# Attention and two MLP layers on one core: the order of work at the layer change, three gate subtracts and one conversion step on other engines

## The chip, the cores and the metric

One core of one Trainium2 chip runs the whole program. The metric is the device time of one execution in microseconds (us), as the median of several runs. The core has five engines, each working through its own queue in order: TensorE (matmuls, PE in the profile), VectorE (DVE), ScalarE (ACT), GpSimd (POOL) and SyncE (SP, which here issues all DMAs).

## The reference

Attention with a compressive memory, whose output of 2304 tokens by 512 goes through two MLP layers. Cut to what is computed:

```python
# q, k, v: 4 x 8 heads x 576 x 64; causal softmax attention 'local', and a memory read 'mem_out'
x = g * mem_out + (1 - g) * local            # -> 2304 x 512
h = x @ w_in                                 # layer one, 512 -> 2048
x = (h * (1 / (1 + exp(-1.702 * h)))) @ w_out
h = x @ w_in2                                # layer two
out = (h * clip(h + 3, 0, 6) / 6) @ w_out2
```

The four weight matrices come as float64, the rest as float32.

## The kernel before

The 2304 tokens are six tiles of 384 (`TILES`, NT = 384), kept transposed, so that a tile is four pieces of 128 x 384 (KD = 4, index kk or d). The hidden dimension is cut in NF = 16 parts, index f. A *unit* is (layer, tile, f): layer one's six tiles with sixteen parts each, then layer two's. The function `moe` walks through the units. For each unit it issues the h product (lines 302 to 304), starts the gate, and then issues the y product (lines 282 to 284) of an earlier unit, so that the gate has time.

Every factor is split into a rounded float32r half and a rest, and a product is three matmuls of 128 x 128 by 128 x 384: weight half by data half, weight rest by data half, weight half by data rest. So h takes 12 matmuls (four quarters kk of three), and y takes 12 (three for each output piece d, summed over f in four banks).

*The gate* of one unit (`gate`) is four instructions: an activation of h on ScalarE (line 254 for layer one, a tanh; 258 for layer two, a relu), a VectorE instruction that multiplies by h (256, 260), a cast on ScalarE to the half `g[:, 0]` (263), and a subtract that gives the rest `g[:, 1]` (265). The subtract is on VectorE for layer one's first tile and on GpSimd for all others (`GLE`).

*The splits of x* (`split_x`, lines 247 and 248) are the same cast on ScalarE and subtract on VectorE, one pair for each quarter. The buffers of the split x exist once, so a split of the next tile waits until the h product of f = 15 has read that quarter. They are asked for by `after_quarter`: for the next tile of layer one and, after layer one's last tile, for layer two's first tile at f = 15; for layer two at f = 12.

*The weights* come as float64 words, and `conv_w` makes a half and a rest of each block of 128 x 512: on VectorE lines 197 and 202 (shift and merge of the two 32-bit words, in place), on GpSimd line 206 (add the constant STEP to the high word read as a float), on ScalarE line 208 (Abs of the low word; part of layer one's are done on VectorE, line 210) and line 212 (Sign of the high word less STEP), on VectorE line 215 (min and multiply), on ScalarE line 222 (cast to the half), and line 225 (the rest; on VectorE for layer two). There are 64 such conversions, 32 for each layer. Layer two's are issued one in every 7 steps of the stream (`PR`; a unit has 8 steps), from layer one's last tile on.

The code makes chains of these steps as generators, which advance by one step at each `chains.step()`. A step of layer two's conversions is kept behind the last gate's instruction on the same engine (`after_gates` with CB = 0). What the code gives is a priority; the program is built with a planner that plays the instructions through with its own durations and fixes the order on each engine, so the order on an engine is not the order of the code.

From layer one's last tile on (`LAG` = 3), y runs three units behind h, h has three banks, and g has four buffers. So when layer one's last h product is issued, y of f = 12 follows, and y of f = 13, 14 and 15 wait in `pend`; they are issued behind h of layer two's f = 0, 1 and 2.

Of the kernel before, what the change touches and what calls it, by code (L numbers as in the profile page):

```python
# [8 lines left out]
F32 = mybir.dt.float32  # L9
F32R = mybir.dt.float32r  # L10
I32 = mybir.dt.int32
AF = mybir.ActivationFunctionType
ALU = mybir.AluOpType
# [6 lines left out]
KD = DM // 128  # L20
NF = DFF // 128
# [18 lines left out]
DPIN = (1, 0, 0, 0, 0, 1)  # L40
NR = ((1,), (1,), (1,), (1,), (1,), (1,))
GLE = (0, 1, 1, 1, 1, 1, 1)
XEV = (0,)
PC = ((1, 6, 11), 8)
W0 = (2, 3)
# [18 lines left out]
STEP = 768.0  # L64
# [12 lines left out]
def f32(ap):  # L77
    return ap.bitcast(F32)
# [26 lines left out]
def attention_moe_kernel(ctx: ExitStack, tc: tile.TileContext, qk0, sk0, sk1, vm0, vm1, bb, w1, w2, out):  # L105
    nc = tc.nc
    PE, ACT, DVE, POOL, SP = nc.tensor, nc.scalar, nc.vector, nc.gpsimd, nc.sync

    const = ctx.enter_context(tc.tile_pool(name="const", bufs=1))
# [8 lines left out]
    chains = Chains()  # L118
# [11 lines left out]
    gated = {"DVE": [], "ACT": [], "POOL": []}  # L130
# [51 lines left out]
    def conv_w():  # L182

        n = w_at[1]
        key = layer, f, a = w_jobs[n]
        if n >= 4 and w_jobs[n - 4] in w_gen:
            chains.finish(w_gen[w_jobs[n - 4]])
        w_at[1] += 1
        load_w(w_at[1])
        if layer == 0:  # L190
            load_w(min(2 * NF, w_at[1] + AHEAD))
        z = 2 if layer == 1 else int(2 * f + a >= 2 * PRE)
        words = w_raw.pop(key).rearrange("p (n two) -> p n two", two=2)
        lo, hi = words[:, :, 0], words[:, :, 1]

        def chain():
            first = DVE.tensor_scalar(
                out=lo, in0=lo, scalar1=29, scalar2=0x40000000, op0=ALU.logical_shift_right, op1=ALU.bitwise_or
            )
            if PIN[layer]:  # L200
                tc.keep_in_program_order(first)
            DVE.scalar_tensor_tensor(
                out=lo, in0=hi, scalar=3, in1=lo, op0=ALU.logical_shift_left, op1=ALU.bitwise_xor
            )
            yield
            POOL.tensor_scalar(out=f32(hi), in0=f32(hi), scalar1=STEP, scalar2=1.0, op0=ALU.add, op1=ALU.mult)  # L206
            if (2 * f + a) % ABS[z][1] < ABS[z][0]:
                ACT.activation(out=f32(lo), in_=f32(lo), func=AF.Abs)
            else:
                DVE.tensor_scalar(out=lo, in0=lo, scalar1=0x7FFFFFFF, scalar2=None, op0=ALU.bitwise_and)  # L210
            yield
            ACT.activation(out=f32(hi), in_=f32(hi), func=AF.Sign, bias=step_down[:, 0:1])  # L212
            yield
            x = temp(layer, f, a)
            DVE.scalar_tensor_tensor(  # L215
                out=x, in0=f32(lo), scalar=BIG, in1=f32(hi), op0=ALU.min, op1=ALU.mult
            )
            pool, tag = slot(layer, f, a)
            t = pool.tile([128, 2, DM], F32R, tag=tag, bufs=1, name=f"w{f}{a}")
            wt[key] = t  # L220
            yield
            ACT.copy(out=t[:, 0], in_=x)  # L222
            yield
            e = "DVE" if (2 * f + a) % WLE[z][1] < WLE[z][0] else "POOL"
            {"DVE": DVE, "POOL": POOL}[e].tensor_tensor(out=t[:, 1], in0=x, in1=f32(t[:, 0]), op=ALU.subtract)  # L225

        w_gen[key] = chains.start(after_gates(chain(), CB[layer]))

    def convert_to(n):
# [14 lines left out]
    def split_x(key, kk):  # L244
        r = xr.pop((key, kk))
        t = xp.tile([128, 2, NT], F32R, tag=f"xs{kk}", name=f"xs{kk}")
        ACT.copy(out=t[:, 0], in_=r)  # L247
        DVE.tensor_tensor(out=t[:, 1], in0=r, in1=f32(t[:, 0]), op=ALU.subtract)
        xs[key, kk] = t

    def gate(layer, ti, h, g):
        t = gp.tile([128, NT], F32, tag="t", bufs=GB, name="t")
        if layer == 0:
            ACT.activation(out=t, in_=h, func=AF.Tanh, scale=0.851)  # L254
            yield
            d = DVE.scalar_tensor_tensor(out=t, in0=t, scalar=1.0, in1=h, op0=ALU.add, op1=ALU.mult)  # L256
        else:
            ACT.activation(out=t, in_=h, func=AF.Relu, bias=three[:, 0:1])  # L258
            yield
            d = DVE.scalar_tensor_tensor(out=t, in0=t, scalar=6.0, in1=h, op0=ALU.min, op1=ALU.mult)  # L260
        gated["DVE"].append(d.ins)
        yield
        gated["ACT"].append(ACT.copy(out=g[:, 0], in_=t).ins)  # L263
        yield
        d = (DVE, POOL)[GLE[ti if layer == 0 else -1]].tensor_tensor(out=g[:, 1], in0=t, in1=f32(g[:, 0]), op=ALU.subtract)  # L265
        gated[("DVE", "POOL")[GLE[ti if layer == 0 else -1]]].append(d.ins)

    def moe(units, before_h, after_quarter, finish):


        pend = []

        def emit_y():
            layer, ti, f, g, gen = pend.pop(0)
            chains.finish(gen)
            w = need_w(layer, f, 1)
            if f == 0:
                for d in range(KD):
                    ys[d] = psy.tile([128, NT], F32, tag=f"y{d}", name=f"y{d}")
            for d in range(KD):  # L280
                o = d * 128
                PE.matmul(ys[d], lhsT=w[:, 0, o:o + 128], rhs=g[:, 0], start=(f == 0), stop=False)  # L282
                PE.matmul(ys[d], lhsT=w[:, 1, o:o + 128], rhs=g[:, 0], start=False, stop=False)  # L283
                PE.matmul(ys[d], lhsT=w[:, 0, o:o + 128], rhs=g[:, 1], start=False, stop=(f == NF - 1))  # L284
                if f == NF - 1:
                    finish(layer, ti, d, ys[d])
                chains.step()
                if d == KD - 1 and layer == 0 and ti == LAST:
                    load_w(2 * (NF + EARLY + f + 1))
                yield layer, ti, f  # L290

        ys = [None] * KD
        for layer, ti, f in units:
            before_h(layer, ti, f)
            w = need_w(layer, f, 0)
            h = phase["h"].tile([128, NT], F32, tag=phase["tag"], bufs=phase["bufs"], name="h")
            for kk in range(KD):
                x = xs[(layer, ti), kk]
                c = kk * 128
                behind = phase["behind"]() if kk % EVERY == 0 else None  # L300
                with tc.issue_after(behind) if behind is not None else ExitStack():
                    PE.matmul(h, lhsT=w[:, 0, c:c + 128], rhs=x[:, 0], start=(kk == 0), stop=False)  # L302
                PE.matmul(h, lhsT=w[:, 1, c:c + 128], rhs=x[:, 0], start=False, stop=False)  # L303
                PE.matmul(h, lhsT=w[:, 0, c:c + 128], rhs=x[:, 1], start=False, stop=(kk == KD - 1))  # L304
                after_quarter(layer, ti, f, kk)
                if kk < KD - 1:
                    chains.step()
                    yield layer, ti, f
            g = phase["g"].tile([128, 2, NT], F32R, tag="g", bufs=phase["lag"] + 1, name="g")
            gen = chains.start(gate(layer, ti, h, g))  # L310
            chains.step()
            yield layer, ti, f
            pend.append((layer, ti, f, g, gen))
            while len(pend) > phase["lag"]:
                yield from emit_y()
        while pend:
            yield from emit_y()
# [420 lines left out]
    with ExitStack():  # L738
# [3 lines left out]
        for _ in range(WARM):  # L742
# [6 lines left out]
            out=mask[:, 384:512], in_=mask[:, 384:512], pattern=[[-1, 128]], compare_op=ALU.is_ge,  # L749
# [6 lines left out]
        POOL.memset(three, 3.0)  # L756
        step_down = const.tile([128, 1], F32, name="step_down")
        POOL.memset(step_down, -STEP)

        gall = const.tile([128, 4, H], F32, name="gall")  # L760
        omg = const.tile([128, H], F32, name="omg")
# [16 lines left out]
        LAST = len(TILES) - 1  # L778
        units = [(layer, ti, f) for layer in range(2) for ti in range(len(TILES)) for f in range(NF)]
# [10 lines left out]
        def before_h(layer, ti, f):  # L790
            if layer == 0 and f == NF - 1 and ti < LAST:
                pump(1 << 30)
            if layer == 1 and f == 2:
                load_x2(ti + 1)

        def after_quarter(layer, ti, f, kk):
            if layer == 0 and f == NF - 1:
                split_x((0, ti + 1) if ti < LAST else (1, 0), kk)
            elif layer == 1 and f == NF - 4 and ti < LAST:
                split_x((1, ti + 1), kk)  # L800

        def load_x2(ti):
            if ti > LAST:
# [3 lines left out]
                move(4, out=r, in_=x2d[ti, d])  # L807
                xr[(1, ti), d] = r

        stream = moe(units, before_h, after_quarter, finish)  # L810

        with tc.tile_pool(name="ap", bufs=2) as ap:
            temps[:] = [ap, TWB[0]]
# [12 lines left out]
            qi, ti = 0, 0  # L826
            for layer, t, f in stream:
                if t != ti:
                    ti, qi = t, 0
# [79 lines left out]
```

## Time and profile before

| | us |
|---|---|
| median of 3 runs | 1082.98 (1082.46 to 1084.0) |
| the profiled execution, its own time | 1084.36 |
| its span, first to last instruction | 1082.5 |
| mean granted TensorE clock | 0.98 of full speed |
| TensorE busy | 1033.4 (95%) |
| VectorE busy | 510.2 (47%) |
| ScalarE busy | 498.8 (46%) |
| GpSimd busy | 399.1 (37%) |

The times of the profile count from the first instruction. In the stretch up to about 600 us attention and layer one run together; from there to about 740 us layer one's last tile and layer two's first tile run while layer two's weights are converted; after that layer two has only its products and gates. "PEclk" is the clock that was granted to TensorE, as a share of 2.4 GHz; a matmul's end is modelled, and matmuls overlap, so the number of matmuls in a stretch says more than TensorE's busy share. A gate or conversion is followed by its line number through the engines. "Idle before" is time in which the engine stood still just ahead of an instruction, and the name behind the arrow is what it waited for last.

### The profile page before, as it was taken

The page shows a single profiled execution, that of the slowest core. Times are in us where ns is not written, and L with a number is a line of the kernel's source. Part 1 is how long each engine was busy: PE and PEld are TensorE (multiplying, and loading weights), DVE is VectorE, ACT ScalarE, POOL GpSimd, SP SyncE. Part 2 cuts the span into 40 slices and gives each one's busy share as a digit, 9 for nine tenths or more (in the row PEclk, how much of TensorE's full clock was granted, in tenths as well). Part 3 has the DMA queues.
Part 4 walks back from the last instruction along what each step waited for, and adds up shares of the span by engine and source line. Part 5 has one row for each costly group of instructions (what it writes and reads, how often), then busy time and mean ns, then how long its engine had stood idle before and what let it go on. Part 6 is the DMA issues. An engine that isn't in the chain of part 4 may idle for free. (4 is left out here: it accounts for less than half of the span.)

```text
span 1082.5 us, 16719 instructions
## 1 busy us (share of the span) xinstructions
PE 1033.4 (95%) x6153; PEld 940.3 (87%) x6153; DVE 510.2 (47%) x1372; ACT 498.8 (46%) x1152; POOL 399.1 (37%) x444
## 2 busy tenths in 40 slices
PE   7877888999999999999999997998999999999998
PEld 4566766888888888888889997998999999999998
DVE  6999997344544443333444598873121121211210
ACT  6757655334454454433333566764233232332322
POOL 4778765223333333222322454543222222222221
PEclk9888998999999999999999998999999999999999
DMA  6643321211121110211110684001010010100000
GB/s 227 239 158 103 127 69 36 68 45 59 28 76 37 38 55 25 59 30 60 30 30 16 246 324 140 30 1 59 1 31 30 1 59 1 31 30 1 30 1 29
DMA packets 29280, 71.91 MB, mean 66 GB/s; under 512 B 3600, under 2 KB 12816, under 8 KB 29200
## 3 DMA queue, kind: packets, MB, share of 16 engines
q1 hardware_dynamic: 29200, 70.86, 19.7%
q8 instruction: 48, 0.79, 0.3%
q14 instruction: 32, 0.26, 0.1%
HBM read 61.41 MB, written 9.44 MB: 65 GB/s over the span
## 5 line engine op out<-in xcount | busy, mean ns | idle before, releaser
L265 POOL TENSOR_TENSOR g<-t,g 128x384 fp32r<-128x384 f32 x176 | 185.1, 1052 | 473.1 <-ACT g L263 448.5
L302 PE MATMUL h<-xs,w 128*128 128x384 f32 x768 | 267.1, 348 | 16.1 <-DVE t L256 8.1
L282 PE MATMUL y<-g,w 128*128 128x384 f32 x768 | 260.4, 340 | 3.4 <-ACT g L263 3.3
L303 PE MATMUL h<-xs,w 128*128 128x384 f32 x768 | 260.1, 339 | 0.3 <-DVE w L225 0.3
L304 PE MATMUL h<-xs,w 128*128 128x384 f32 x768 | 260.3, 339 | 0.0
L283 PE MATMUL y<-g,w 128*128 128x384 f32 x768 | 259.2, 337 | 0.0
L284 PE MATMUL y<-g,w 128*128 128x384 f32 x768 | 244.1, 339 | 0.6 <-POOL g L265 0.6
L260 DVE SCALAR_TENSOR_TENSOR t<-t,h 128x384 f32<-128x384 f32 x96 | 53.1, 553 | 273.2 <-ACT t L258 273.2
L302 PEld LDWEIGHTS h<-xs,w 128*128 128x128 f32 x768 | 146.3, 191 | 24.7 <-DVE t L256 12.6
L282 PEld LDWEIGHTS y<-g,w 128*128 128x128 f32 x768 | 145.1, 189 | 7.0 <-ACT g L263 4.6
L284 PEld LDWEIGHTS y<-g,w 128*128 128x128 f32 x768 | 142.3, 188 | 6.7 <-issue 4.1
L303 PEld LDWEIGHTS h<-xs,w 128*128 128x128 f32 x768 | 146.6, 191 | 1.4 <-issue 0.8
L304 PEld LDWEIGHTS h<-xs,w 128*128 128x128 f32 x768 | 146.0, 190 | 1.1 <-issue 0.5
L283 PEld LDWEIGHTS y<-g,w 128*128 128x128 f32 x768 | 145.1, 189 | 1.4 <-issue 1.3
L263 ACT CAST g<-t 128x384 fp32r<-128x384 f32 x192 | 98.4, 513 | 95.1 <-DVE t L260 49.2
L258 ACT ACTIVATE t<-h,three 128x384 f32<-128x384 f32 x96 | 55.7, 580 | 170.5 <-PE h L304 170.5
L454 POOL TENSOR_SCALAR p<-p,st,omg 128x128 f32<-128x128 f32 (+3 forms) x128 | 91.8, 729 | 99.3 <-DVE st L450 44.7
L446 ACT ACTIVATE p<-s,st 128x256 f32<-128x256 f32 (+4 forms) x160 | 82.4, 521 | 69.6 <-DVE st L441 57.5
L441 DVE CUSTOM_DVE_ANT_0 s<-s,mask 128x128 f32<-128x128 f32 (+3 forms) x144 | 72.6, 526 | 85.0 <-PE s L381 84.1
L256 DVE SCALAR_TENSOR_TENSOR t<-t,h 128x384 f32<-128x384 f32 x96 | 52.7, 550 | 74.5 <-ACT t L254 70.3
L381 PE MATMUL s<-qk 64*128 64x256 f32 (+5 forms) x384 | 72.3, 466 | 12.2 <-issue 3.5
L254 ACT ACTIVATE t<-h 128x384 f32<-128x384 f32 x96 | 46.7, 490 | 67.9 <-PE h L304 65.1
(79 smaller groups left out, 1103.5 us busy)
## 6 DMA issues: line engine op xcount, KB each, us to landing
r<-in_w_dram SPq DMA_DIRECT2D x64, 512.0 KB, 6.2
vm<-in_vm_dram SPq DMA_DIRECT2D x16, 386.0 KB, 3.0
qk<-in_qk_dram SPq DMA_DIRECT2D x16, 384.0 KB, 3.5
qk<-in_sk_dram SPq DMA_DIRECT2D x32, 192.0 KB, 3.3
x2d<-yo SPq DMA_DIRECT2D x24, 192.0 KB, 1.9
xr<-x2d SPq DMA_DIRECT2D x24, 192.0 KB, 3.1
out_dram<-yo SPq DMA_DIRECT2D x24, 192.0 KB, 1.9
vm<-in_vm_dram SPq DMA_DIRECT2D x16, 258.0 KB, 2.7
```

The source lines that it names most:

```text
L263: gated["ACT"].append(ACT.copy(out=g[:, 0], in_=t).ins)
L265: d = (DVE, POOL)[GLE[ti if layer == 0 else -1]].tensor_tensor(out=g[:, 1], in0=t, in1=f32(g[:, 0]), op=ALU.subtract)
L282: PE.matmul(ys[d], lhsT=w[:, 0, o:o + 128], rhs=g[:, 0], start=(f == 0), stop=False)
L283: PE.matmul(ys[d], lhsT=w[:, 1, o:o + 128], rhs=g[:, 0], start=False, stop=False)
L284: PE.matmul(ys[d], lhsT=w[:, 0, o:o + 128], rhs=g[:, 1], start=False, stop=(f == NF - 1))
L302: PE.matmul(h, lhsT=w[:, 0, c:c + 128], rhs=x[:, 0], start=(kk == 0), stop=False)
L303: PE.matmul(h, lhsT=w[:, 1, c:c + 128], rhs=x[:, 0], start=False, stop=False)
L304: PE.matmul(h, lhsT=w[:, 0, c:c + 128], rhs=x[:, 1], start=False, stop=(kk == KD - 1))
L381: ins = PE.matmul(out, **args).ins
L441: DVE.tensor_tensor_reduce(out=o, in0=o, in1=m, scale=-SCALE, scalar=init, op0=ALU.add, op1=ALU.min, accum_out=out)
L446: return ACT.activation(out=dst, in_=o, func=AF.Exp, scale=-1.0, bias=m, accum_out=s)
L454: (DVE, POOL)[e[norms[0] % len(e)]].tensor_scalar(out=dst, in0=dst, scalar1=s, scalar2=w, op0=ALU.mult, op1=ALU.mult)
```

## The change

Three edits. (1) The splits of x for layer two's first tile are no longer asked for by the quarters of layer one's last h product. When the stream comes to layer two's first unit, a new function `between` asks for all four, and then all y products that still wait (f = 13, 14, 15) are issued, ahead of layer two's first h product. (2) In layer one's last tile the gate's subtract of the last three parts (`GLL` = 3, so f = 13, 14, 15) is on VectorE and no longer on GpSimd. (3) In layer two's conversions the step constant is added on ScalarE, as an Identity activation with a bias tile, and no longer on GpSimd; the bias tile is set once at the start.

```diff
+GLL = 3
...
-            POOL.tensor_scalar(out=f32(hi), in0=f32(hi), scalar1=STEP, scalar2=1.0, op0=ALU.add, op1=ALU.mult)
+            if layer == 0:
+                POOL.tensor_scalar(out=f32(hi), in0=f32(hi), scalar1=STEP, scalar2=1.0, op0=ALU.add, op1=ALU.mult)
+            else:
+                ACT.activation(out=f32(hi), in_=f32(hi), func=AF.Identity, bias=step_up[:, 0:1])
...
-    def gate(layer, ti, h, g):
+    def gate(layer, ti, f, h, g):
...
-        d = (DVE, POOL)[GLE[ti if layer == 0 else -1]].tensor_tensor(out=g[:, 1], in0=t, in1=f32(g[:, 0]), op=ALU.subtract)
-        gated[("DVE", "POOL")[GLE[ti if layer == 0 else -1]]].append(d.ins)
+        e = "POOL" if GLE[ti if layer == 0 else -1] and not (layer == 0 and ti == LAST and f >= NF - GLL) else "DVE"
+        d = {"DVE": DVE, "POOL": POOL}[e].tensor_tensor(out=g[:, 1], in0=t, in1=f32(g[:, 0]), op=ALU.subtract)
+        gated[e].append(d.ins)
...
         for layer, ti, f in units:
+            if (layer, ti, f) == (1, 0, 0):
+                between()
+                while pend:
+                    yield from emit_y()
             before_h(layer, ti, f)
...
+        step_up = const.tile([128, 1], F32, name="step_up")
+        POOL.memset(step_up, STEP)
...
         def after_quarter(layer, ti, f, kk):
-            if layer == 0 and f == NF - 1:
-                split_x((0, ti + 1) if ti < LAST else (1, 0), kk)
+            if layer == 0 and f == NF - 1 and ti < LAST:
+                split_x((0, ti + 1), kk)
...
+        def between():
+
+            for kk in range(KD):
+                split_x((1, 0), kk)
```

## Rows read from the trace of the kernel before

**Rows 1.** Windows: busy us of PE, PEld, DVE, ACT, POOL; clock, DMA, GB/s

```profile
616.00:738.00 122.00, 113.86 (x632) 110.54 (x631) 102.84 (x150) 84.27 (x151) 61.81 (x57) 0.97 0.35 125
...
654.00:674.00 20.00, 14.15 (x65) 12.43 (x64) 15.37 (x24) 12.81 (x24) 8.63 (x8) 0.83 0.39 129
...
730.00:742.00 12.00, 9.03 (x39) 7.82 (x38) 8.59 (x14) 7.60 (x16) 3.88 (x4) 0.86 0.10 27
...
742.00:1082.00 340.00, 337.14 (x1945) 336.82 (x1944) 52.48 (x96) 106.05 (x201) 81.97 (x81) 1.00 0.07 23
```

**Rows 2.** Timeline of TensorE: start, duration, instruction, in brackets idle before, releaser

```profile
656.53 0.33 PE L304 MATMUL h<-xs,w 128*128 128x384 f32 x1
...
660.54 0.45 PE L282 MATMUL y<-g,w 128*128 128x384 f32 x1 [1.60 <-ACT g L263]
...
661.74 0.44 PE L284 MATMUL y<-g,w 128*128 128x384 f32 x1 [0.57 <-POOL g L265]
...
666.02 0.69 PE L302 MATMUL h<-xs,w 128*128 128x384 f32 x1 [3.67 <-ACT xs L247]
...
669.69 0.52 PE L304 MATMUL h<-xs,w 128*128 128x384 f32 x1
...
671.33 0.33 PE L284 MATMUL y<-g,w 128*128 128x384 f32 x1
```

**Rows 3.** Timeline of ScalarE, same columns

```profile
668.43 0.49 ACT L247 CAST xs<-xr 128x384 fp32r<-128x384 f32 x1
...
668.83 0.48 ACT L254 ACTIVATE t<-h 128x384 f32<-128x384 f32 x1
```

**Rows 4.** Waits of VectorE, 616 to 738 us; total us, times, longest

```profile
DVE wt L215 <- ACT r L212: 11.4, 9, 2.3
...
DVE t L260 <- ACT t L258: 2.9, 4, 1.3
```

**Rows 5.** Waits of ScalarE, 616 to 738 us

```profile
ACT r L212 <- POOL r L206: 6.0, 10, 1.0
```

**Rows 6.** Groups by line, 616 to 738 us; busy us, mean ns, idle before

```profile
L202 DVE SCALAR_TENSOR_TENSOR r<-r 128x512 int32<-128x512 int32 x30 | 35.3, 1190 | 0.1
...
L225 DVE TENSOR_TENSOR w<-wt,w 128x512 fp32r<-128x512 f32 x30 | 23.9, 806 | 2.7 <-ACT w L222 2.7
...
L212 ACT ACTIVATE r<-r,step_down 128x512 f32<-128x512 f32 x30 | 22.8, 768 | 6.2 <-POOL r L206 6.0
...
L215 DVE SCALAR_TENSOR_TENSOR wt<-r 128x512 f32<-128x512 f32 x30 | 22.6, 760 | 11.4 <-ACT r L212 11.4
```

**Rows 7.** Four lines alone, 616 to 738 us; duration min/median/max, ns

```profile
L202 DVE SCALAR_TENSOR_TENSOR r<-r x30: 678/1498/1511, 617.3 to 731.8; 128x512 int32<-128x512 int32 x30
...
L206 POOL TENSOR_SCALAR r<-r x30: 642/1025/1110, 618.8 to 733.4; 128x512 f32<-128x512 f32 x30
...
L215 DVE SCALAR_TENSOR_TENSOR wt<-r x30: 677/684/1137, 622.6 to 734.8; 128x512 f32<-128x512 f32 x30
...
L225 DVE TENSOR_TENSOR w<-wt,w x30: 678/682/1503, 625.5 to 736.2; 128x512 fp32r<-128x512 f32 x30
```

**Rows 8.** Timeline of all engines around one conversion

```profile
655.30 1.50 DVE L202 SCALAR_TENSOR_TENSOR r<-r 128x512 int32<-128x512 int32 x1
...
656.84 0.68 ACT L208 ACTIVATE r<-r 128x512 f32<-128x512 f32 x1 [0.81 <-DVE r L202]
...
657.95 0.75 ACT L212 ACTIVATE r<-r,step_down 128x512 f32<-128x512 f32 x1 [0.43 <-POOL r L206]
...
660.57 1.11 POOL L265 TENSOR_TENSOR g<-t,g 128x384 fp32r<-128x384 f32 x1 [2.66 <-ACT g L263]
...
660.75 1.49 DVE L202 SCALAR_TENSOR_TENSOR r<-r 128x512 int32<-128x512 int32 x1
```

**Rows 9.** Groups by line over the whole span

```profile
L265 DVE TENSOR_TENSOR g<-t,g 128x384 fp32r<-128x384 f32 x16 | 11.6, 728 | 0.0
...
L611 ACT ACT_TABLE_LOAD x1 | 1.3, 1283 | 0.7 <-PEq L892 0.7
```

More of the change, by code (lines that the diff above doesn't have):

```diff
@@ L264, in gate, with moe @@
         yield
-        d = (DVE, POOL)[GLE[ti if layer == 0 else -1]].tensor_tensor(out=g[:, 1], in0=t, in1=f32(g[:, 0]), op=ALU.subtract)
-        gated[("DVE", "POOL")[GLE[ti if layer == 0 else -1]]].append(d.ins)
-    def moe(units, before_h, after_quarter, finish):
+        e = "POOL" if GLE[ti if layer == 0 else -1] and not (layer == 0 and ti == LAST and f >= NF - GLL) else "DVE"
+        d = {"DVE": DVE, "POOL": POOL}[e].tensor_tensor(out=g[:, 1], in0=t, in1=f32(g[:, 0]), op=ALU.subtract)
+        gated[e].append(d.ins)
+    def moe(units, before_h, after_quarter, between, finish):
         pend = []
@@ L309, in moe @@
             g = phase["g"].tile([128, 2, NT], F32R, tag="g", bufs=phase["lag"] + 1, name="g")
-            gen = chains.start(gate(layer, ti, h, g))
+            gen = chains.start(gate(layer, ti, f, h, g))
             chains.step()
@@ L808, in load_x2 @@
                 xr[(1, ti), d] = r
-        stream = moe(units, before_h, after_quarter, finish)
+        stream = moe(units, before_h, after_quarter, between, finish)
         with tc.tile_pool(name="ap", bufs=2) as ap:
```

## The prediction, made before the changed kernel ran

> **What bounds the kernel now.** I read the page first (busy shares and the 40 slices), then the windows of the stretch that the slices show ragged, then who TensorE waits for there, then the timeline of TensorE, ScalarE and of one weight conversion, and last who VectorE and ScalarE wait for.
>
> In the windows the reader is to see where matmuls are missing. From 742 us to the end TensorE issues 1945 matmuls in 340 us, 0.175 us each, and is busy for 337.14 us [rows 1]: nothing that the change touches acts there. At that rate the 65 matmuls of 654 to 674 us are worth 11.4 us, so 8.6 us are lost; the 39 of 730 to 742 us are worth 6.8, so 5.2 are lost. 13.8 us in all: that is the whole prize. The first place is the change from layer one to layer two, the second the end of layer two's first token tile. Of the 8.6 us, 5.85 are idle time (20 less 14.15); the rest is slow running: the granted clock of that window is 0.83, a mixture of the 1.2 and 2.4 GHz levels, and a matmul at 669.69 lasts 0.52 us against 0.33 before the gap [rows 1, 2].
>
> TensorE's waits name the gates' casts, a g rest and the splits of x [rows 2], and those are late because their engines are behind. The last h product of layer one issues its last matmul at 656.53; its tanh starts on ScalarE at 668.83, 12 us later [rows 2, 3]. The largest waits of VectorE and ScalarE from 616 to 738 us are for each other and for GpSimd; TensorE is not among their releasers [rows 4, 5]. So in this stretch the three vector engines set the pace, VectorE first (102.84 us busy of 122), ScalarE next (84.27), and TensorE stalls when their lag has used up its three banks and four g buffers. A stall saved in TensorE's order is kept only if the vector engines' work gets shorter too.
>
> **The step constant on ScalarE (L206).** Thirty conversions of layer two fall into the stretch [rows 6]. What goes from VectorE: the instructions with two inputs in SBUF that stood still behind L206. L225 has a mean of 806 ns and L215 of 760 [rows 6], with medians of 682 and 684, which I take for the undisturbed time [rows 7]; excess 30 x 0.124 + 30 x 0.076 = 3.7 + 2.3 = 6.0 us. That this is GpSimd's doing is read from pairs like that of rows 8, where L202 (0.68 at its shortest [rows 7]) started 0.18 us after a g rest on GpSimd and took 1.49. A part of the 6.0 belongs to the g rests, which stay, so 6.0 is the upper end and 3 the lower. I take -5.
>
> What comes to ScalarE: no Identity with a bias is in the trace; the nearest row is L212, the Sign with the same bias operand on the same strided words, 768 ns [rows 6], of which 0.1 overlaps with the next (the split at 668.43 lasts 0.49, the tanh behind it begins at 668.83 [rows 3]). 30 x 0.66 = 20 us more work on an engine that has 122 - 84.27 = 37.7 us free. On the path it counts only where VectorE waits for the Sign: nine times, 11.4 us [rows 4]. Before, from the end of L202 (655.30 + 1.50 = 656.80) to the end of the Sign (657.95 + 0.75 = 658.70) it was 1.90 us, with GpSimd's step, 1.03 us in the median, beside the Abs [rows 7, 8]. After, three ScalarE instructions follow each other: 0.66, the Abs with 0.68 - 0.1 [rows 8], the Sign with 0.77, and a hop of 0.04 make 2.05, so +0.15; where GpSimd's step took its shortest, 0.64 [rows 7], instead of 1.03, +0.5. Nine times 0.15 to 0.5 is 1.4 to 4.5; I take +2.5. The other 21 push gates and casts back on ScalarE's queue; VectorE waits there for gates 2.9 us in four waits [rows 4], which can grow by 0.65 each, 2.6; I take +1, and keep 30 x 0.5 = 15 us as the upper end of the whole edit, for a ScalarE that becomes the path throughout. Its 6.0 us of waits for GpSimd [rows 5] are already in the 1.90.
>
> The Trainium skill (ScalarE: Activation LUTs, What ACT_TABLE_LOAD costs) prices an activation with a pointer bias at about 280 ns plus 0.833 per element, 707 ns for 512; by it the 20 us would be an estimated 18. The same page (Table sets: the hidden batching unit) says that cheap functions, identity among them, are in every set; no run here shows Identity, and only one table load is in the trace [rows 9]. If it did need its own set, two loads of 1.283 us for each of 32 conversions would be 82 us; I leave that out of the range.
>
> Sum of this edit: -5 + 2.5 + 1 = -1.5 (ends -6 and +15).
>
> **Three g rests on VectorE.** The rests of f = 13, 14 and 15 leave GpSimd and cost VectorE 728 ns each by the sixteen that it already does [rows 9], some 0.65 of it its own after overlap: +1.95. In exchange the conversion step L202 that ran into such a rest (1.49 against 0.68 [rows 7, 8]) loses 0.8 us, for two of the three: -1.6. TensorE's wait of 0.57 for GpSimd's rest [rows 2] goes, and what is late next is the cast itself. The first conversion afterwards no longer queues behind the last rest on GpSimd. I take -1 (ends -2.2 and +2, the latter if the collisions only move to another instruction).
>
> **The y products ahead of layer two's first h.** Three groups of 12 matmuls (3 x 12 x 0.175 = 6.3 us) now stand before the first h, and the four splits are issued after the last gate's first steps instead of ahead of its tanh. No instruction is added; x's splits are 4 casts and 4 subtracts either way. Moved past: layer one's last four y evictions and their four stores on SP now come before layer two's first gates instead of among them; SP has no weight load left to issue behind them, since the jobs run out with y 12. Loads of x for the next tile, which reuse the split's source, slip with the splits by some 2 us and are needed only at 738.
>
> Before, TensorE ran 4 matmuls from 660.54 until the wait before 666.02, then y and h mixed, at first at the low clock; from 660.54 to 671.33 there are 23 [rows 2]. After: y 13 waits as now for its cast (660.54 [rows 2]); y 14 for the next, one gate period of 4 us later (664.5); y 15 for the last, whose tanh is now ahead of four casts of 0.4 us each (0.49 less the overlap [rows 3]), so 668.83 - 1.6 = 667.2, and its cast ends at about 669. The 36 matmuls end near 671.4, with x split meanwhile: 13 matmuls ahead, 13 x 0.175 = 2.3 us. Four h products in a row then give the gates of layer two 8 us of lead before y needs the first one. I keep -2 (ends -4 and +3, the latter in the second rival). The memset of step_up lies in the start, beside other work: 0.
>
> **Sum.** -1.5 - 1 - 2 = -4.5 us. The profiled execution took 1084.36 (span 1082.5 and 1.86 around it), 1.38 above the median of the runs shown, 1082.98. 1084.36 - 4.5 = 1079.9, as a median of runs 1078.5.
>
> **Rivals.**
> *ScalarE takes VectorE's place* (slower). Place: each conversion's Identity, Abs and Sign in one queue with the gates. ScalarE goes from 84 to about 104 us of 122, VectorE falls to about 97; in-order queues that release each other at such loads lose time at each hand-over. For it: in the rhythm of one conversion at a time [rows 8] the step is on the loop L202, Sign, L215, L202 and not beside it. Against it: VectorE waits for the Sign in only 9 of 30 [rows 4]. It decides once more than about half of the conversions have it on the path: 30 x 0.35 = 10.5 less 5 saved on VectorE, +5.5: 1088.5; with the y order as a gain of 2, 1086.5.
>
> *The drained pipeline* (slower). Layer two's first h can't start before y 15, and y 15 hangs on the last gate, the latest of all. If that gate still starts at 668.83, y 15 ends near 673 and the first h starts there, not at 666.02 [rows 2]. Until its product is done at 675 the vector engines have only the conversions issued meanwhile, 2.3 of them (one in 7 steps of the stream, 16 steps between the two gates); at 2.5 us of VectorE each (four instructions of some 0.6) that is 6 us behind a gate that ends at 670, too little or just enough with the hand-overs: 1.5 to 4 us of waiting for TensorE, which they don't have now. It decides from a last gate later than 668: about 1086. For it: that gate's lag of 12 us; against it, the casts that no longer stand before it.
>
> *Handed back* (no change). The lag of the gates grows again through layer two's first tile, and TensorE stalls at 730 to 742 us for what it gained at 666. For it: the vector engines hardly wait for TensorE [rows 4, 5]. Then what remains is what the conversions save, near zero: 1082.5. That the change does not do what it says belongs here: all orders are made anew by a planner that knows durations but places every instruction again, and a gain of 2 us can vanish in another order.
>
> *Collisions fall away too* (faster). L202's mean of 1190 ns against 678 at the shortest is 15 us of standing still over 30 [rows 6, 7], nearly all from g rests that start just as it does. If the new order shifts the two apart, half of it goes: 1073.
>
> **How the numbers follow.** Forecast 0.42; collisions also fall away 0.06; handed back 0.17; ScalarE the path 0.25; drained pipeline 0.10. Runs of this kernel differ by about 0.2%, 2.2 us, so that is what counts as no change. Faster 0.48, same 0.17, slower 0.35. The forecast's own range is 1075 to 1081; the whole, with the collisions below it and a ScalarE path above, 1072 to 1090. Cases of both signs hold most of the chance, and the range is wide because the terms are small beside the ends of one edit, -6 and +15.
>
> **What would show it.** L215 and L225 back at 0.68 us in the mean and no L206 on GpSimd in layer two: the first term. VectorE's wait for the Sign near 14 us in the stretch: right; above 20: ScalarE is the path. Three groups of y between 660 and 671.5 us and no h before 670: the third edit; the first h after 675: the drained pipeline. Matmuls lost in 730 to 742 us: 5.2 now; if they grow by what the first place saves, it was handed back. The prediction is wrong in its ground if the vector engines show idle time for TensorE in the stretch.

## The result and the profile after

The changed kernel takes 1073.82 us (median of 4 runs, 1071.15 to 1076.01) against 1082.72 before (4 runs, 1082.27 to 1084.0): ratio 0.9915, interval 0.989 to 0.994. That is 8.9 us less, where 4.5 were forecast; 1073.82 lies inside the stated range of 1072 to 1090 but below the forecast's own 1075 to 1081, and nearest to the rival in which collisions fall away too (1073). The profiled execution was the fastest of its four, 1071.15, with a span of 1069.3; the other three took 1073.18 to 1076.01, and what they lost beyond it stands in no trace.

The windows answer to [rows 1], with the same columns; the matmuls are worth 0.175 us each as before.

```profile
616.00:738.00 122.00, 119.16 (x688) 118.84 (x687) 98.10 (x158) 104.88 (x191) 34.95 (x28) 1.00 0.37 129
654.00:674.00 20.00, 17.16 (x99) 16.84 (x99) 15.97 (x32) 18.30 (x36) 0.00 (x0) 1.00 0.48 159
730.00:742.00 12.00, 12.00 (x71) 12.00 (x70) 1.66 (x3) 5.11 (x11) 3.04 (x3) 1.00 0.10 36
742.00:1069.00 327.00, 323.99 (x1870) 323.67 (x1868) 50.82 (x93) 100.20 (x190) 77.94 (x77) 1.00 0.06 21
```

From 654 to 674 us there are 99 matmuls and not 65, so 2.7 us are lost instead of 8.6; from 730 to 742 there are 71 and not 39, and nothing is lost where 5.2 were. The granted clock of 654 to 674 us is 1.00, not 0.83: TensorE's only long wait there did not bring it down in this execution. The tail runs at the old rate. So 11 of the 13.8 us that were to be had came back at these two places in this execution, which is 13.2 us shorter than the profiled one of before; the medians are 8.9 apart.

The lines of the stretch answer to [rows 6]; the numbers moved: L203 is the word merge (L202 before), L219 the multiply (L215), L229 the rest of the weight (L225), L216 the Sign (L212), and L210 is the new Identity. VectorE first (L270 are the three g rests that came to it), then ScalarE; after the bar busy us and mean ns.

```profile
L229 DVE TENSOR_TENSOR w<-wt,w 128x512 fp32r<-128x512 f32 x30 | 24.5, 822 | 2.1 <-ACT w L226 2.0
L219 DVE SCALAR_TENSOR_TENSOR wt<-r 128x512 f32<-128x512 f32 x30 | 24.2, 807 | 7.0 <-ACT r L216 6.9
L203 DVE SCALAR_TENSOR_TENSOR r<-r 128x512 int32<-128x512 int32 x30 | 23.4, 794 | 0.2
L270 DVE TENSOR_TENSOR g<-t,g 128x384 fp32r<-128x384 f32 x3 | 1.6, 548 | 0.6 <-ACT g L267 0.6
L210 ACT ACTIVATE r<-r,step_up 128x512 f32<-128x512 f32 x30 | 23.0, 768 | 2.9 <-DVE r L203 2.8
L216 ACT ACTIVATE r<-r,step_down 128x512 f32<-128x512 f32 x30 | 22.7, 761 | 0.0
```

The reader is to see where VectorE's relief sits. The merge fell from a mean of 1190 ns to 794; the multiply and the rest of the weight did not fall but rose, from 760 to 807 and from 806 to 822. Over 0.682 us undisturbed, the three stood still for 30 x (0.508 + 0.078 + 0.124) = 21.3 us before and for 30 x (0.112 + 0.125 + 0.140) = 11.3 us after. What is left is all from the g rests, since they are the only work that GpSimd still has in the stretch. Such a pair, first GpSimd's row, then VectorE's, where the rest of the weight starts 0.08 us behind a g rest and takes 1.51 us; and the other way round, a g rest that takes 2.60 us while VectorE works through three instructions with two inputs in SBUF in a row (L203, L229, L219, to 642.80 us):

```profile
650.21 1.04 POOL L270 TENSOR_TENSOR g<-t,g 128x384 fp32r<-128x384 f32 x1 [3.43 <-ACT g L267]
```

```profile
650.29 1.51 DVE L229 TENSOR_TENSOR w<-wt,w 128x512 fp32r<-128x512 f32 x1
```

```profile
641.09 2.60 POOL L270 TENSOR_TENSOR g<-t,g 128x384 fp32r<-128x384 f32 x1 [3.58 <-ACT g L267]
```

The Trainium skill (SBUF — State Buffer, Who interferes with whom) states this as a rule: a VectorE instruction with two inputs in SBUF contends with a GpSimd instruction that reads SBUF, over a shared pair of ports that is an exclusive lock. The traces agree, with 1.5 us for 0.68 on the one side and 2.60 for 1.04 on the other.

Who waits for whom, answering to [rows 4, 5]: the first fence is VectorE, the second ScalarE (both 616 to 738 us), the third is a row of the kernel before that was not shown above.

```profile
DVE t L264 <- ACT t L262: 9.1, 5, 3.4
DVE wt L219 <- ACT r L216: 6.9, 8, 3.2
```

```profile
ACT t L262 <- PE h L313: 6.9, 4, 2.4
...
ACT r L210 <- DVE r L203: 2.8, 5, 0.8
```

```profile
ACT r L208 <- DVE r L202: 21.5, 19, 2.1
```

Before, ScalarE stood 19 times, 21.5 us, at the head of its queue with an Abs that waited for the merge, and the gates behind it stood too; now it is 5 times, 2.8 us. And ScalarE now waits for TensorE's h, which it did not before: the vector engines have caught up. The last tanh of layer one starts at 657.67, 2.5 us after its product, where it was 12.

There was a second meeting of g rests and step before, in GpSimd's own queue, which is worked through in order. When a step stood there behind a g rest, it came late, most of all where the rest itself still waited for its cast. Rows of the kernel before, a merge on VectorE and then the rest and the step on GpSimd:

```profile
649.60 0.69 DVE L202 SCALAR_TENSOR_TENSOR r<-r 128x512 int32<-128x512 int32 x1
```

```profile
650.93 1.44 POOL L265 TENSOR_TENSOR g<-t,g 128x384 fp32r<-128x384 f32 x1 [1.73 <-ACT g L263]
652.34 1.11 POOL L206 TENSOR_SCALAR r<-r 128x512 f32<-128x512 f32 x1
```

The merge ended at 650.29 and its step began 2.05 us later; an undisturbed step begins after 0.09. By the timelines 9 of the 30 steps stood behind a g rest so, 11.7 us beyond that 0.09 in all, and 19 of the 30 merges ran into one, 15 us. With the step on ScalarE the second meeting is gone, and the first is rarer.

One loss is new. TensorE's timeline at the layer change, and ScalarE's, answering to [rows 2, 3]:

```profile
664.91 0.33 PE L311 MATMUL h<-xs,w 128*128 128x384 f32 x1
...
669.42 0.34 PE L313 MATMUL h<-xs,w 128*128 128x384 f32 x1
672.60 0.44 PE L311 MATMUL h<-xs,w 128*128 128x384 f32 x1 [2.84 <-DVE t L264]
```

```profile
657.67 0.47 ACT L258 ACTIVATE t<-h 128x384 f32<-128x384 f32 x1
...
665.57 0.47 ACT L333 ACTIVATE yo<-y 128x384 f32<-128x384 f32 x1
...
671.26 1.02 ACT L262 ACTIVATE t<-h,three 128x384 f32<-128x384 f32 x2
```

Layer two's h products now come in a row, but for nine matmuls of the first, which the planner put ahead of y 15 (from 661.27 us). The first three fill the three banks, and the fourth waits 2.84 us for the first gate, whose relu starts only at 671.26, 5.7 us after its product: ScalarE has put steps of three conversions and the four evictions of layer one's last y ahead of it.

### The profile page after: what moved, and what is told of

It is laid out like the page before. It is cut to its first block, busy times and chain, and to the rows that moved or that the text cites. A ratio compares the mean times of both kernels' runs of the same rounds, so it can differ in the third digit from the quotient of the medians.

```text
span 1069.3 us, 16682 instructions
## 1 busy us (share of the span) xinstructions
PE 1026.5 (96%) x6153; PEld 938.0 (88%) x6153; DVE 501.7 (47%) x1375; ACT 514.6 (48%) x1184; POOL 369.1 (35%) x410
## 4 chain that ended last, share of the span: by engine, by line
PE 83%; DVE 11%; ACT 3%; issue 1%; DMA 1%; SPq 0%; POOL 0%; DVEq 0%; ACTq 0%
PE h L311 12%; PE y L287 12%; PE y L288 12%; PE y L289 12%; PE h L312 11%; PE h L313 11%; PE o L390 5%; PE s L390 5%; PE t L405 2%; DVE r L203 2%; DVE s L450 2%; DVE r L198 1%; DVE wtemp L219 1%; ACT p L455 1%; PE mem L375 1%
## 5 line engine op out<-in xcount | busy, mean ns | idle before, releaser
L270 POOL TENSOR_TENSOR g<-t,g 128x384 fp32r<-128x384 f32 x173 | 183.1, 1059 | 502.4 <-ACT g L267 478.6
L463 POOL TENSOR_SCALAR p<-p,st,omg 128x128 f32<-128x128 f32 (+3 forms) x128 | 94.2, 748 | 100.1 <-DVE st L459 46.5
```

Source lines behind the costliest of these rows:

```text
L270: d = {"DVE": DVE, "POOL": POOL}[e].tensor_tensor(out=g[:, 1], in0=t, in1=f32(g[:, 0]), op=ALU.subtract)
L463: (DVE, POOL)[e[norms[0] % len(e)]].tensor_scalar(out=dst, in0=dst, scalar1=s, scalar2=w, op0=ALU.mult, op1=ALU.mult)
```

## The experiments

Three readings were open. *A*: the gain is the step constant's, which no longer keeps GpSimd and VectorE in each other's way; as *A1* it is the old step's own hold on the shared port, as *A2* it is which of VectorE's instructions runs into the g rests. *B*: the gain is the order at the layer change. *C*: each edit only lets the planner draw a new order. The kernel before was run beside all of them; its median was between 1082.88 and 1083.51 in the three sittings.

**One edit alone, and the two order edits together.**

```diff
# id_only: the kernel before, and
-            POOL.tensor_scalar(out=f32(hi), in0=f32(hi), scalar1=STEP, scalar2=1.0, ...)
+            (layer two) ACT.activation(out=f32(hi), in_=f32(hi), func=AF.Identity, bias=step_up[:, 0:1])
# y_only: the kernel before with between() and the waiting y ahead; GLL = 0, step on GpSimd
# rest_only: the kernel before with GLL = 3 alone
# y_and_rest: the changed kernel with the step back on GpSimd
```

> The kernel before with the step constant of layer two's conversions on ScalarE alone; y order and g rests as before. Theory A (GpSimd's step is what makes VectorE's word merge L202 run into g rests; the gain comes from this edit): 1073 to 1077 us, mean of the merge in the stretch 616 to 738 us below 0.9 us (1.19 before), gate lag of layer one's last unit below 6 us (12 before). Theory B (the gain comes from the y products ahead and the splits after the gate): 1081 to 1086, merge near 1.19, lag near 12. Theory C (each edit only re-rolls the planner's order): anything, and not additive with the others.

> The kernel before with the waiting y products ahead of layer two's first h and the splits after them in the code, nothing else. Theory A: 1080 to 1086 us, gate lag at the layer change still 9 us or more, merge near 1.19 us. Theory B: 1073 to 1078, no stall over 1 us at the layer change. Theory C: not foretold, but the lag before 650 us, where nothing of the edit acts, would differ from 10 us.

> The kernel before with only the last three g rests of layer one on VectorE. Theories A and B: 1081 to 1085 us, since it touches three instructions of the stretch. Theory C: could move by 4 us or more either way.

> The changed kernel with the step constant back on GpSimd: both order edits without the ScalarE edit. Theory A: 1080 to 1086 us, merge near 1.19 us and the lag at the layer change 9 us or more. Theory B: 1073 to 1077, as with all three edits. Theory C: not foretold.

| kernel | median us | ratio to before, interval |
|---|---|---|
| id_only | 1071.16 | 0.9892 (0.9879 to 0.9906) |
| y_only | 1083.6 | 1.0007 (0.9997 to 1.0016) |
| rest_only | 1080.55 | 0.9978 (0.9969 to 0.9987) |
| y_and_rest | 1079.65 | 0.9967 (0.9954 to 0.9979) |

The Identity alone brings 12.1 us (1083.27 less 1071.16), more than all three edits, and 1.8 us more than the range of A. The y order alone brings nothing, the three rests 2.7 us, both without the Identity 3.6 (these two came out some 0.4 us below A's ranges). B falls. C's sign is not there in y_only: the gates ahead of the edit's place are late by as much as before (the tanh of f = 13 starts 10.39 us after its product in both). The windows and VectorE's lines of the Identity alone:

```profile
654.00:674.00 20.00, 19.87 (x114) 19.40 (x112) 18.18 (x28) 14.80 (x28) 5.72 (x5) 1.00 0.38 120
674.00:730.00 56.00, 54.53 (x310) 53.66 (x311) 47.14 (x72) 50.53 (x94) 16.54 (x14) 1.00 0.07 23
```

```profile
L219 DVE SCALAR_TENSOR_TENSOR wt<-r 128x512 f32<-128x512 f32 x30 | 25.9, 864 | 4.4 <-ACT r L216 4.3
L229 DVE TENSOR_TENSOR w<-wt,w 128x512 fp32r<-128x512 f32 x30 | 25.4, 850 | 4.1 <-ACT w L226 4.1
L203 DVE SCALAR_TENSOR_TENSOR r<-r 128x512 int32<-128x512 int32 x30 | 24.1, 821 | 0.2
```

With 114 matmuls from 654 to 674 us (the fastest versions below have 117 and 118) almost nothing is lost at the layer change although its order is the old one, so no stall of order was there to be mended: the splits were late because the gates were. From 674 to 730 us some 15 matmuls, 2.6 us, are still missing. The merge's mean is 821 ns. In y_only TensorE waits for gate after gate, with the y products where the edit puts them:

```profile
659.62 0.45 PE L284 MATMUL y<-g,w 128*128 128x384 f32 x1 [1.60 <-ACT g L264]
...
663.66 0.45 PE L284 MATMUL y<-g,w 128*128 128x384 f32 x1 [0.81 <-ACT g L264]
...
669.58 0.44 PE L284 MATMUL y<-g,w 128*128 128x384 f32 x1 [1.97 <-ACT g L264]
673.72 1.33 PE L286 MATMUL y<-g,w 128*128 128x384 f32 x3 [2.81 <-POOL g L267]
```

These are the casts of y 13, 14 and 15, as the prediction placed them (660.5, 664.5, 669), and the rest of y 15 on GpSimd last. The stall changed its name and grew, and what it cost came back at the end of the tile. Windows of y_only, and the middle one of before:

```profile
654.00:674.00 20.00, 11.60 (x59) 9.63 (x58) 16.29 (x26) 12.01 (x23) 10.58 (x8) 0.96 0.38 120
674.00:730.00 56.00, 56.00 (x310) 56.00 (x311) 45.60 (x65) 39.55 (x71) 27.43 (x27) 0.95 0.04 15
730.00:742.00 12.00, 10.43 (x55) 9.79 (x54) 8.94 (x14) 7.57 (x16) 3.81 (x4) 0.95 0.06 20
```

```profile
674.00:730.00 56.00, 55.92 (x323) 55.56 (x322) 46.24 (x69) 39.89 (x72) 27.75 (x26) 1.00 0.04 15
```

Against before that is 6 and 13 matmuls fewer up to 730 us, and 16 more from there to 742.

**Did the old step hold the port, or did the order do it?** In id_pool_busy GpSimd gets a step of the old size back, on a spare tile, at the old moment, with nobody waiting for it; the other four engines keep the same instructions in the same order as in id_only. In step_on_dve the step goes to VectorE instead of ScalarE.

```diff
# id_pool_busy: id_only, and in layer two
+                after(POOL.tensor_scalar(out=mask, in0=mask, scalar1=STEP, scalar2=1.0, ...).ins, [merged.ins])
# step_on_dve: id_only with
-                ACT.activation(out=f32(hi), in_=f32(hi), func=AF.Identity, bias=step_up[:, 0:1])
+                DVE.tensor_scalar(out=f32(hi), in0=f32(hi), scalar1=STEP, scalar2=1.0, op0=ALU.add, op1=ALU.mult)
```

> The kernel with the Identity on ScalarE alone, and beside it on GpSimd, in each conversion of layer two, a step of the same size on a spare tile that starts at the end of the word merge, as the old step did; nobody waits for it. TensorE, VectorE, ScalarE and SyncE keep the same order of instructions. Theory A1 (the old step holding the port it shares with VectorE was the cost): 1076 to 1083 us, VectorE stands still 8 us or more longer in the stretch. Theory A2 (the new order and phase of the g rests against the merge is what gained): 1071 to 1074, at most 5 us more of standing still.

> The kernel before with the step constant of layer two's conversions on VectorE instead of GpSimd (some 0.34 us each by the shift of the same size, 30 x 0.34 = 10 us more on VectorE in the stretch; ScalarE as before). Theory A1 (it only had to leave GpSimd): 1074 to 1080 us. Theory A2 (it had to come to ScalarE, whose order sets when the g rests start): 1080 to 1090.

id_pool_busy takes 1074.62 us (0.9929, 0.9916 to 0.9941), between the two expectations: 3.5 us above id_only, out of 12.1. Its VectorE lines and GpSimd's spare step:

```profile
L225 DVE SCALAR_TENSOR_TENSOR wt<-r 128x512 f32<-128x512 f32 x30 | 28.7, 958 | 3.6 <-ACT r L222 3.6
L212 POOL TENSOR_SCALAR mask<-mask 128x512 f32<-128x512 f32 x30 | 28.6, 955 | 9.6 <-DVE r L203 9.2
L235 DVE TENSOR_TENSOR w<-wt,w 128x512 fp32r<-128x512 f32 x30 | 26.7, 892 | 3.0 <-ACT w L232 3.0
L203 DVE SCALAR_TENSOR_TENSOR r<-r 128x512 int32<-128x512 int32 x30 | 24.9, 849 | 0.2
```

By the means VectorE stands still for 19.6 us here (5.0 in the merge, 8.3 and 6.3 in the others), 14.7 in id_only (4.2, 5.5 and 5.0) and 21.3 before (15.2, 2.3 and 3.7). So a step on GpSimd that nobody waits for is worth 4.9 us of standing still and 3.5 us of time (3.9, if each version is held against the kernel before of its own sitting; g rests now queue behind the spare step too, so not all of it need be the port): A1 is true and the smaller part. The other 8.6 us came although the sum of standing still is nearly that of before: the merge, which ScalarE's queue waits for, is hardly hit any more, and the hits fell on the later steps. But no conversion waits for GpSimd's queue any more either, and this run does not part the two.

step_on_dve takes 1075.55 us (0.9933, 0.9919 to 0.9946). VectorE does 30 more instructions of 555 ns in the stretch, and the kernel still gains 7.3 us (1082.88 less 1075.55):

```profile
L203 DVE SCALAR_TENSOR_TENSOR r<-r 128x512 int32<-128x512 int32 x29 | 29.5, 1022 | 0.0
L210 DVE TENSOR_SCALAR r<-r 128x512 f32<-128x512 f32 x30 | 16.3, 555 | 0.3
```

The merge, at 1022 ns, keeps two thirds of its standing still (10.2 of 15.2 us), so its relief alone is not the whole gain. It was enough for the step to leave GpSimd; ScalarE, with more room, is the better place.

**No g rest on GpSimd in the stretch.** If A2 holds, the collisions can be taken away with the step left on GpSimd, by moving the other partner.

```diff
# rests_dve: the kernel before with
-        ... (DVE, POOL)[GLE[ti if layer == 0 else -1]]
+        e = "POOL" if GLE[ti if layer == 0 else -1] and not ((layer, ti) in ((0, LAST), (1, 0))) else "DVE"
# id_rests_dve: the same and the Identity on ScalarE
```

> The kernel before with all g rests of layer one's last and layer two's first tile on VectorE (32 of them, 0.47 us of VectorE each, 15 us), the step constant still on GpSimd. Theory A2 (the price was where VectorE stood still: the word merge behind a g rest): no such collision is left, 16 us of standing still go, lag below 8 us at layer one's last gate, 1072 to 1080 us. Theory A1 (GpSimd's step holding the port, or ScalarE's chain through GpSimd): that step stays, VectorE has as much work as before, 1081 to 1088.

> The Identity on ScalarE and all 32 of those g rests on VectorE, y order as before: GpSimd does nothing in the stretch and VectorE never stands still behind it. If every collision costs: 1067 to 1069 us, no matmul lost from 616 to 742. If VectorE's added 15 us cost as much as the 12 to 14.5 us of standing still that go: 1070 to 1073.

rests_dve takes 1068.13 us (0.9862, 0.9846 to 0.9878), better than the better expectation, with the Identity nowhere. Windows and VectorE's lines:

```profile
654.00:674.00 20.00, 20.00 (x117) 20.00 (x116) 19.96 (x35) 17.18 (x33) 5.40 (x6) 1.00 0.41 139
...
730.00:742.00 12.00, 12.00 (x71) 12.00 (x71) 1.66 (x3) 4.97 (x10) 3.04 (x3) 1.00 0.18 66
```

```profile
L216 DVE SCALAR_TENSOR_TENSOR wt<-r 128x512 f32<-128x512 f32 x30 | 23.2, 773 | 1.3 <-ACT r L213 1.2
L226 DVE TENSOR_TENSOR w<-wt,w 128x512 fp32r<-128x512 f32 x30 | 22.4, 756 | 1.0 <-ACT w L223 0.9
L203 DVE SCALAR_TENSOR_TENSOR r<-r 128x512 int32<-128x512 int32 x30 | 21.3, 709 | 0.2
L267 DVE TENSOR_TENSOR g<-t,g 128x384 fp32r<-128x384 f32 x29 | 17.9, 619 | 2.5 <-ACT g L264 2.5
```

No matmul is missing at either place. The old step still stands in VectorE's way for some 5.7 us (0.8, 2.7 and 2.2 by the means), and VectorE is busier than before (105.78 us of 122 against 102.84); both cost nothing now. What had cost was that g rests and steps met on GpSimd: the merge behind the g rest, and the step behind it in the queue. Moving the rests ends both, moving the step ends the second and most of the first, and no run ends only one (step_on_dve comes nearest); so how the price divides between them is not shown. With the Identity as well (id_rests_dve) it is 1067.5 us (0.9853, 0.9837 to 0.9868), the fastest version, 6.3 us below the changed kernel; that it beats rests_dve is within their spread (1066.35 to 1067.95 against 1067.25 to 1069.2).

**What the y order does once the gates keep up.** id_and_rest is the changed kernel without the y order, id_and_y without the three rests, all_fourth_bank the changed kernel with a fourth bank.

```diff
# id_and_rest: after_quarter as before, no between()
# id_and_y: GLL = 0
# all_fourth_bank: the changed kernel, and
+            if (layer, ti, f) == (1, 0, 0):
+                h = psy.tile([128, NT], F32, tag="h", bufs=1, name="h")
```

> The changed kernel without the y order: Identity on ScalarE and three g rests on VectorE. If the y order is what costs: 1069 to 1072 us. If the rests cost: 1073 to 1076.

> The changed kernel without the g rests on VectorE: Identity on ScalarE and the y products ahead. If the y order is what costs the 2.7 us between the Identity alone (1071.2) and all three edits (1073.8): 1073 to 1076. If the g rests on VectorE cost it: 1071 to 1072.

> The changed kernel, with layer two's first h product in the bank that attention has left free, so that four h products in a row have four banks. If the y order costs because the fourth h waits 2.8 us for a bank: 1069 to 1072. If it costs because conversions and evictions are bunched ahead of layer two's first gates on ScalarE: 1073 to 1075, and y of layer two's first unit waits for its cast instead.

id_and_rest takes 1068.11 us (0.9862, 0.9849 to 0.9876), id_and_y 1074.08 (0.9915, 0.9902 to 0.9929). So the y order costs 2.9 us with the Identity (1074.08 against 1071.16) and 5.7 with the Identity and the rests (1073.82 against 1068.11; 3.1 between the two profiled executions), although alone it cost nothing. TensorE's longest wait around the layer change, in id_and_y and then in all_fourth_bank; in id_and_rest TensorE has no wait there at all and is busy for the whole stretch:

```profile
PE h L311 <- DVE t L264: 4.8, 1, 4.8
```

```profile
PE h L314 <- DVE t L264: 1.7, 1, 1.7
```

```profile
616.00:738.00 122.00, 122.00 (x706) 122.00 (x705) 99.83 (x159) 106.06 (x195) 35.24 (x29) 1.00 0.37 132
```

With the fourth bank the kernel takes 1071.06 us (0.9886, 0.9871 to 0.9902), in the range that was expected if the bank is the cost: the next h now waits, and 1.7 us instead of 2.84. That is not firm: the interval overlaps the changed kernel's (0.989 to 0.994), and the two profiled executions are alike (1071.10 and 1071.15). The remaining 3 us to id_and_rest fit the late first gates, which the extra bank leaves as they are (the first relu 5.75 us after its product, against 5.67 in the changed kernel and 1.47 in id_and_rest); that they are late because conversions and evictions stand ahead of them is read from ScalarE's timeline and was not tried by itself.

**All versions together.** Over the ten that do not join the Identity with the y order, the time falls with the mean of the merge in the stretch: 1190 ns at about 1083 us, 1083 at 1080.55 (rest_only), 1063 at 1079.65 (y_and_rest), 1022 at 1075.55, 849 at 1074.62, 821 at 1071.16, 711 at 1068.11 (id_and_rest). The sum of standing still of the three steps does not order them so: it is 18.7 us in y_and_rest and 19.6 in id_pool_busy, which is 5 us faster. This is a pattern over versions whose orders all differ, and the step queues behind g rests in those above 1079 us alone.

## Why the prediction was right, and where not

The sign was right and the time lies in the stated range, but near its lower end, at a rival that was given 0.06. The three terms were not right: alone they measure -12.1, -2.7 and nothing, and a loss of the y order in company cancels a part. That the sum came out within the range is in good part luck.

**What bounds the kernel: right.** The vector engines' lag set the pace, and TensorE's stalls were its trace. id_and_rest and rests_dve, without a missing matmul, took the whole prize and 1 to 1.6 us more than the 13.8: 14.8 us (1082.88 less 1068.11) and 15.4 (1083.51 less 1068.13). The rate of 0.175 us, from a stretch with 2.9 us of idle time, was a little slow; the full stretch of id_and_rest has 122/706 = 0.173. One sign of the prediction spoke against its ground all the same, idle time of the vector engines for TensorE: ScalarE waits 6.9 us for h in the changed kernel. Before it did not; the sign could not tell a wrong ground from vector engines that have caught up.

**The step constant: mis-sized, -1.5 forecast, -12.1 measured alone.** The -5 for the old step's collisions is near what a spare step brings (4.9 us of standing still in id_pool_busy), but it did not come from where it was said to: the multiply and the rest of the weight did not go back to 0.68 us, their standing still rose from 6.0 to 8.0 us, as the g rests now ran into them. The failing sentence is "A part of the 6.0 belongs to the g rests, which stay": they stay, but no longer in front of the merge. The 15 us of the merge were seen and put into a rival at 0.06, as if only luck could move them. The other term left out is GpSimd's queue, named only for the first conversion after the last rest: the 1.90 us from merge to Sign were read from one conversion [rows 8] whose step started at once, while 9 of 30 stood behind a g rest, 11.7 us in all. The prediction also took a hit to cost the same wherever it falls; behind the merge stood ScalarE, 21.5 us at the head of its queue, and behind it the gates, while 12.0 us of standing still, 11.1 of them in the later steps, cost no matmul in id_and_rest. On the other side the costs were too high. The Identity came out as estimated (768 ns, not the 707 that the prediction quotes; ScalarE 104.88 us busy of 122 against 104; still one table load in the trace), but VectorE's wait for the Sign fell to 6.9 us where 14 were foretold. Its wait for the gates' relu rose from 2.9 to 9.1 us, past the 2.6 that were allowed for. Why the planner's new order keeps the merge clear of the g rests is not settled: the runs show that it does, with the step on ScalarE (821 ns) and less with the step on VectorE (1022), not which step of its plan did it.

**Three g rests on VectorE: right in kind, -1 forecast, -2.7 alone (1083.27 less 1080.55) and -3.0 beside the Identity (1071.16 less 1068.11).** The second is 2.7 too, if each is held against the kernel before of its own sitting. As forecast, merges lost their hits: in rest_only the mean fell from 1190 to 1083 ns, 3.2 us over 30. The rest takes VectorE some 0.55 us in the stretch, not the 0.73 taken from layer one's first tile.

**The y products ahead: wrong sign, -2 forecast, none alone, +2.9 to +5.7 in company.** The forecast argued from TensorE's position at 671.5 us, against its own sentence that such a gain is kept only if the vector engines get shorter work. Its sign, no h before 670 us, did not come: the first h starts at 661.27. The rival of the drained pipeline named the cost, 1.5 to 4 us, but another cause: not vector engines waiting for the first h, but three banks filled in a row ahead of gates that start 5.7 us late, as far as the traces show it.

**The rivals.** ScalarE as the path: refuted, it is busy for 106.06 us of 122 in id_and_rest with no matmul lost. Handed back: refuted for the whole, since no matmul is missing from 730 to 742 us; the y order alone did the reverse, it lost up to 730 us and gained from there to 742. Collisions fall away too: this is what happened (15.2 us of standing still in the merge before, 3.4 after), and with it the wait in GpSimd's queue, which no rival named.

## What to carry to other kernels

When an instruction's mean is far above its shortest time, ask first what stands behind it: here 12.0 us of standing still, nearly all late in the chain, cost no matmul (id_and_rest), and 21.3 us, most of it where another engine's queue waited, went with 15 us of loss. Where two kinds of work meet on one engine, moving either can cure it, as the step and the g rests did here; look for both prices, the collision with the other engine and the place in the engine's own queue, since busy shares show neither. And a stall of TensorE that comes from late suppliers is not mended by feeding TensorE in another order; test such an edit again, alone, once the suppliers keep up.

## What had not been expected of the hardware

A GpSimd instruction can be stretched as far as VectorE's: a g rest took 2.60 us for 1.04 while VectorE ran one instruction with two SBUF inputs after another. And the wait of 2.84 us in the changed kernel left the granted clock at 1.00 in its window, while the stalls of before, 1.60, 0.57 and 3.67 us within 8 us [rows 2], went with 0.83. A wait of 4.8 us in id_and_y was not so lucky: the clock was 0.52 of full speed from 674 to 676 us, behind the wait, and 0.63 to 678, with 14 matmuls in 4 us.
